# Fewer, area-weighted filler matmuls and softmax denominators spread by DMA, in a planned two-layer attention and MLP kernel

## The chip, the cores and the metric

The kernel runs on one core of one Trainium2 chip. The metric is the device time of one execution in microseconds (us). "Before" stands for the kernel as it is and "after" for the kernel with the change.

## The reference

Two layers are applied to one sequence of 2048 rows with 448 columns. Each layer is an attention block of 16 heads (28 columns each) and a mixer block with shifted groups of columns and an MLP of 1792 hidden columns. Each sub-block has a residual sum. Weights are the same in both layers.

```python
def _A_ref(x, wqkv, wo):                       # B=1, S=2048, D=448, H=16, Dh=28
    q, k, v = qkv of (x @ wqkv) by head
    p = softmax(einsum("bhqd,bhkd->bhqk", q, k) * Dh ** -0.5)
    return concat_heads(einsum("bhqk,bhkd->bhqd", p, v)) @ wo

def _B_ref(x, w1, w2, w3, w4):                 # F=1792
    h = gelu(layernorm(x) @ w1)
    hs = concat([h0 shifted by 1, h1 by -1, h2 by 2, h3 by -2]) @ w2   # four groups of 112 columns
    x1 = x + hs
    return x1 + gelu(layernorm(x1) @ w3) @ w4

for layer in range(2):
    x = x + _A_ref(layernorm(x), A_wqkv, A_wo)
    x = x + _B_ref(layernorm(x), B_w1, B_w2, B_w3, B_w4)
```

## The kernel before, in words

**A planner writes the order.** The kernel's Python holds tasks (generators such as `t_scores`, `t_exp`, `t_pv`, `t_norm`, `t_mixA`, `t_mixB`). Each task yields operations with an engine, a planned duration, and the tiles it reads and writes. `Sched.run` places them one after the other in planned time: the operation that can start first goes first, with priorities. The result is a fixed list for each of the five queues (TensorE `pe`, ScalarE `act`, VectorE `dve`, GpSimd `pool`, SyncE `sp`); each queue executes its list strictly in order and waits on semaphores where data come from another engine. So a planned duration that is wrong never makes the result wrong, but it puts operations at places in a queue where they are waited for.

**Filler.** `keep_pe_busy` looks at each gap in PE's planned list. Where the recent use of PE (planned busy time in the last `WIN` = 4.0 us) is at most `TARGET` = 0.8, it adds a filler: four matmuls of 256 columns on 32-column tiles of the array, into bank 6 or 7 of PSUM when it is free. Nobody reads what they write. In the list of instructions they are L1608.

**Attention.** Scores for four heads of a group (`g`) stand on four row tiles of the array (32 rows each, L1129). A unit of three or two PSUM banks (0 to 2 and 3 to 4) is turned into probabilities by one ACT instruction (L1204). The PV matmuls (L692, four column tiles) add into bank 5. A segment is one chunk of query rows (512, or 256 at the end), one group of four heads, and a range of key tiles; there are 64 segments. `ORDER` lists the ranges: the first chunks go over the keys in parts, since not all keys are there yet. At the end of a segment, VectorE moves bank 5 out, before the next segment's PV can start. Where a segment isn't its chunk's last one, the sum goes to DRAM (`uscr`) and comes back at the next part (`t_uload`), multiplied by a factor `fct` for the new maximum.

**Denominators.** Column 28 of each head's values is 1, so row 28 of each head's 32 rows of the sum is the softmax denominator. In the 36 final segments `t_norm` picks these rows with fp32 matmuls (`e28`), inverts them on VectorE (`rs`, L1335), turns them with another fp32 matmul (`identf`), copies them (`rT`, L1338), spreads them over the head's rows with fp32 matmuls (`selq`), and multiplies (L1342) into `otn`. An fp32 matmul is two records in the profile. The tile `u` (one buffer `u_sb`) is held from the copy out of bank 5 to this product; the part that is read back has one buffer, `uin`. Before the matmuls `t_norm` waits for `op_done`, the output projection of the chunk before, because `otn` has one buffer.

**After attention.** `t_outproj` multiplies by `wo` and adds to `x_res`. `t_mixA` and `t_mixB` are the mixer and the MLP for the tiles of a chunk: statistics on VectorE, the normalisation on GpSimd (`norm`, L845, into one of six `xn` tiles), a transposing DMA on SP (L850, `xT<-xn`), matmuls (L701), gelu on ACT (L1453 and L1569, each with a change of ACT's table). `t_ln1_l1` then normalises for the next layer, stores to `xnd`, and `load_xT` (L938) reads it back transposed for the projections `k_proj`, `q_proj`, `v_proj`. The projections square K and Q on GpSimd (L953, into one of three `sq` tiles) to bound the maximum of the scores.

Of the kernel before, what the change touches and what calls it, by code (L numbers as in the profile page):

```python
# [7 lines left out]
ALU = mybir.AluOpType  # L8
# [166 lines left out]
class Sched:  # L175
    LAT = 0.2
    EARLY = 0.25
    WIN = 4.0
    TARGET = 0.8
# [88 lines left out]
    def keep_pe_busy(self, until):  # L268
# [3 lines left out]
        while self.cur["pe"] + dur + 0.12 < until:  # L272
            t = self.cur["pe"]
            self.recent = [(a, b) for (a, b) in self.recent if b > t - self.WIN]
            used = sum(b - max(a, t - self.WIN) for (a, b) in self.recent)
# [15 lines left out]
            self.recent.append((t, t + dur))  # L291
# [4 lines left out]
    def run(self):  # L296
        P = self.P
        while True:
# [132 lines left out]
TR_T = 4.0  # L431
TRL_T = 6.0
# [21 lines left out]
def build_kernel(nc, A_x, A_wqkv, A_wo, B_x, B_w1, B_w2, B_w3, B_w4, out, n_layers=2):  # L454
    S = A_x.shape[1]
    D = 448
# [19 lines left out]
    NXN = 6  # L476
# [105 lines left out]
    with st:  # L582
# [39 lines left out]
        sq = sb("sq", [128, 3, 512], BF16)  # L622
# [18 lines left out]
        selq = sb("selq", [16, 512], FP32)  # L641
# [13 lines left out]
        SQ = ["sq0", "sq1", "sq2"]  # L655
        xst = h2T[:, :, :].rearrange("p a b -> p (a b)").rearrange("p (t d) -> p t d", d=D)

        def bi(b):
            return int(b[1:])

# [86 lines left out]
        def t_setup():  # L747
# [68 lines left out]
            yield op("dve", 0.5, lambda e: e.tensor_copy(out=selq[:, :].rearrange("p (c r) -> p c r", r=32), in_=identf[0:16, 0:16].unsqueeze(2).to_broadcast([16, 16, 32])),  # L816
# [138 lines left out]
        def k_proj(L, c, g, xt):  # L955
# [13 lines left out]
            if not fast:  # L969
                yield square(si, dst, dk)  # L970
# [8 lines left out]
        def q_proj(L, qc, g, xt):  # L979
# [8 lines left out]
            s = yield ("acq", SQ)  # L988
            si = num(s)
# [10 lines left out]
            if idx == 0 and g == 0:  # L1000
                yield square_first(b, si)
# [7 lines left out]
            else:  # L1009
                yield ("wait", ("bc", L, p0, g))  # L1010
                yield evac()
                yield ("rel", b)
                yield square(si, dst, [qk])
# [8 lines left out]
        def v_proj(L, c, xt):  # L1022
            yield ("wait", ("vinit",))
            for i in range(4):
# [3 lines left out]
                for fc in FCS:  # L1028
                    yield op("pe", c_mm(D), mm4(ps[:, bi(b), 0:D], xT[:, xt, fc, 128 * i:128 * i + 128], wv[:, fc, :], fc == 0, fc == 3),
# [86 lines left out]
        def score_ops(blks, banks):  # L1116
            m = max(len(seg_kb[b_[0]][b_[1]]) for b_ in blks)
            nc_ = len(blks)
            for i in range(m):
                for blk, bank in zip(blks, banks):  # L1120
# [4 lines left out]
                    if i >= len(ktl):  # L1125
# [6 lines left out]
                        reads=[("kT", g, vslot(L, kt)), qk], writes=[(("ps", bank), i) if len(ktl) > 1 else ("ps", bank)], mode="r32")  # L1132
# [118 lines left out]
        def t_pv():  # L1251
            yield ("wait", ("start",))
            yield ("acq", ["b5"])
            for si in range(len(segs)):
# [9 lines left out]
                while todo or dtodo:  # L1264
# [15 lines left out]
                    for kb in batch:  # L1280
                        for i, kt in enumerate(kbs[kb]):
                            vs = vslot(L, kt)
                            for j in range(4):
# [3 lines left out]
                                         reads=[("vaug", vs), (key, s)], writes=[(("ps", 5), j)], mode="col4")  # L1287
# [8 lines left out]

        def t_uload(si):
# [4 lines left out]
            yield ("acq", ["uin"])  # L1302
            k = 4 * (ch % 2) + g
            yield dma("sp", lambda e: e.dma_start(out=uin[:, :], in_=uscr[k]), reads=[("uscr", k)], writes=[("uin",)], t=3.0)
            yield ("sig", ("uin", si))

        def t_norm(si):
# [3 lines left out]
            yield ("acq", ["u"])  # L1311
            if first:
                yield op("dve", c_ps(NW), lambda e: e.tensor_copy(out=u_sb[:, 0:NW], in_=ps[:, 5, 0:NW]), reads=[("ps", 5)], writes=[("u",)])
            else:
                yield ("wait", ("uin", si))
                yield ("wait", ("fct", L, p[1]))
                yield op("dve", c_ps(NW), lambda e: e.scalar_tensor_tensor(out=u_sb[:, 0:NW], in0=uin[:, 0:NW], scalar=fct[:, L, p[1], g:g + 1], in1=ps[:, 5, 0:NW],  # L1317
                                                                            op0=ALU.mult, op1=ALU.add),
                         reads=[("ps", 5), ("uin",), ("fct", L, p[1])], writes=[("u",)])
                yield ("rel", "uin")  # L1320
            yield ("sig", ("ucopied", si))
            if not last:
                k = 4 * (ch % 2) + g
                yield dma("sp", lambda e: e.dma_start(out=uscr[k], in_=u_sb[:, :]), reads=[("u",)], writes=[("uscr", k)], t=3.0)
# [380 lines left out]
```

## Time and profile before

| | before |
|---|---|
| median of 3 runs | 1233.29 us (1232.92 to 1237.69) |
| profiled execution, its own time | 1229.68 us |
| its span, first to last instruction | 1227.9 us |
| PE busy, share of the span | 1115.2 us, 91% |
| ACT busy | 1062.9 us, 87% |
| DVE busy | 463.0 us, 38% |
| POOL busy | 344.4 us, 28% |
| mean granted TensorE clock | 0.947 |

All numbers of one profile come from one execution. PE is TensorE's matmuls, PEld its weight loads, which overlap them; DVE is VectorE, ACT ScalarE, POOL GpSimd, SP SyncE. A row of a group shows line, engine, operation, output and input tile, shapes and count, then busy time in us and the mean of one instruction in ns, then the idle time of that engine just before it and what ended it. A matmul's record includes its way through the array, so busy times of PE are more than the time for which it is filled. In the row PEclk and in tables by stage the granted clock is a share of full speed.

### The profile page before, as it was taken

To read this page: it belongs to the slowest core of one execution; us is meant where nothing else is said; L and a number is where in the kernel's file an instruction comes from. 1 tells how busy PE (TensorE), PEld (TensorE's weight loads), DVE (VectorE), ACT (ScalarE), POOL (GpSimd) and SP (SyncE) were. 2 spreads that over 40 slices of the span, in tenths; PEclk is the share of its full clock that TensorE was granted. 3 is DMA by queue.
4 is the path that set the end of the run, shared out by engine and by line. 5 is a ranking of instruction groups with operands and counts; after the bars stand their busy time and mean duration, and the time that the engine had idled before them with its cause. 6 is when DMAs were issued, how large, how long until landed. Compare 5 with 4: busy or idle time off the path is not lost.

```text
span 1227.9 us, 34609 instructions
## 1 busy us (share of the span) xinstructions
PE 1115.2 (91%) x15881; PEld 482.0 (39%) x15882; DVE 463.0 (38%) x985; ACT 1062.9 (87%) x906; POOL 344.4 (28%) x364
## 2 busy tenths in 40 slices
PE   5778999899989999899978998999989899989988
PEld 2223453344434433234323433354433333434454
DVE  7654212331232325431463343333343323333343
ACT  3767998999999999999968987999587999999942
POOL 4922203313224035510353231101334130341201
PEclk9889999899999999889988999999698999998999
DMA  3384102001010021100231120432211020120000
GB/s 100 79 229 102 49 10 36 6 11 55 18 32 19 2 81 34 31 5 11 76 78 51 32 80 26 108 95 74 43 27 23 2 52 2 42 42 10 11 17 21
DMA packets 90010, 55.95 MB, mean 46 GB/s; under 512 B 63945, under 2 KB 82249, under 8 KB 89865
## 3 DMA queue, kind: packets, MB, share of 16 engines
q1 hardware_dynamic: 86600, 49.27, 15.8%
q0 software_dynamic: 2304, 3.67, 1.2%
q8 instruction: 124, 2.03, 0.7%
q10 hardware_dynamic: 960, 0.80, 0.2%
q14 instruction: 22, 0.17, 0.1%
HBM read 20.30 MB, written 16.52 MB: 30 GB/s over the span
## 4 chain that ended last, share of the span: by engine, by line
PE 45%; ACT 33%; POOL 9%; DVE 8%; DMA 2%; SPq 2%; issue 2%; ACTq 0%; POOLq 0%; DVEq 0%
ACT PT L1204 28%; PE ps L701 21%; PE ps L692 11%; PE ps L1129 11%; POOL xn L845 5%; ACT h2T L1569 3%; PE ps L1608 2%; DVE st L830 1%; ACT hT L1453 1%; DVE h2T L1559 1%; DVE kmaxc L974 1%; ACT L1453 1%; ACT L1569 1%; DMA xT<-xn 1%; DVE x1b L1512 1%
## 5 line engine op out<-in xcount | busy, mean ns | idle before, releaser
L1204 ACT ACTIVATE PT<-ps 128x1536 bf16<-128x1536 f32 (+1 forms) x819 | 942.2, 1279 | 88.8 <-PE ps L1129 77.0
L1129 PE MATMUL ps<-qT,kT 32*128 32x512 bf16 (+1 forms) x2304 | 331.1, 370 | 16.1 <-ACT PT L1204 8.6
L692 PE MATMUL ps<-PT,vaug 128*32 128x512 bf16 (+1 forms) x2304 | 257.5, 374 | 0.8 <-DVE u_sb L1317 0.5
L1129 PEld LDWEIGHTS ps<-qT,kT 32*128 32x128 bf16 x2304 | 81.3, 91 | 285.1 <-ACT PT L1204 210.2
L701 PE MATMUL ps<-xT,w 128*32 128x512 bf16 (+2 forms) x2240 | 179.5, 371 | 11.9 <-DMA xT<-xn 5.3
L1608 PE MATMUL ps<-wq_pad,ident 128*32 128x256 bf16 x3632 | 170.5, 283 | 9.0 <-DVE x1b L1512 3.8
L701 PE MATMUL ps<-w,h2T 128*32 128x448 bf16 x1792 | 121.0, 370 | 10.4 <-ACT h2T L1569 10.4
L1608 PEld LDWEIGHTS ps<-wq_pad,ident 128*32 128x32 bf16 x3632 | 105.3, 99 | 42.7 <-issue 15.3
L1559 DVE CAST h2T<-ps 128x512 bf16<-128x512 f32 (+2 forms) x126 | 73.9, 587 | 113.7 <-PE ps L701 105.9
L692 PEld LDWEIGHTS ps<-PT,vaug 128*32 128x32 bf16 x2304 | 69.8, 96 | 95.7 <-issue 79.5
L701 PEld LDWEIGHTS ps<-xT,w 128*32 128x32 bf16 (+1 forms) x2240 | 60.2, 96 | 70.3 <-issue 43.1
L953 POOL TENSOR_TENSOR sq<-qT 128x512 bf16<-128x512 bf16 x31 | 32.2, 1039 | 141.2 <-DVE qT L996 140.3
L701 PEld LDWEIGHTS ps<-w,h2T 128*32 128x32 bf16 x1792 | 48.5, 99 | 56.0 <-issue 21.2
L836 POOL TENSOR_SCALAR vpe<-mv 128x1 f32<-128x1 f32 (+2 forms) x21 | 4.8, 229 | 229.3 <-DVE mv L831 229.3
L1569 ACT ACTIVATE h2T<-h2T 128x7168 bf16<-128x7168 bf16 (+2 forms) x9 | 45.1, 5016 | 16.0 <-DVE h2T L1559 15.9
L953 POOL TENSOR_TENSOR sq<-kT 128x512 bf16<-128x512 bf16 x31 | 32.2, 1041 | 94.1 <-DVE kT L965 94.0
L1410 POOL TENSOR_SCALAR mst<-mv 128x4 f32<-128x4 f32 (+1 forms) x9 | 2.2, 240 | 197.8 <-DVE mv L831 197.8
L701 PE MATMUL ps<-w,hT 112*32 112x448 bf16 x512 | 39.8, 421 | 18.8 <-ACT hT L1453 15.5
L845 POOL TENSOR_SCALAR xn<-x_res,mv,mst 128x448 bf16<-128x448 f32 x30 | 55.5, 1859 | 1.8 <-DVE mst L1416 1.5
L845 POOL TENSOR_SCALAR xn<-x1b,mv,mst 128x448 bf16<-128x448 f32 x29 | 54.4, 1876 | 1.3
L1516 POOL TENSOR_SCALAR mst<-mv 128x1 f32<-128x1 f32 x32 | 7.2, 226 | 167.9 <-DVE mv L831 167.9
L701 PE MATMUL ps<-xT,wk_pad 128*32 128x512 bf16 x512 | 46.0, 398 | 4.2 <-DVE kmaxc L974 3.5
(131 smaller groups left out, 1096.0 us busy)
## 6 DMA issues: line engine op xcount, KB each, us to landing
uscr<-u_sb SPq DMA_DIRECT2D x28, 256.0 KB, 2.4
uin<-uscr SPq DMA_DIRECT2D x28, 256.0 KB, 2.9
xnd<-xn SPq DMA_DIRECT2D x28, 128.0 KB, 1.7
x_res<-in_A_x_dram POOLq DMA_DIRECT2D x16, 224.0 KB, 2.7
xd<-x_res SPq DMA_DIRECT2D x16, 224.0 KB, 2.2
x_res<-xd SPq DMA_DIRECT2D x16, 224.0 KB, 3.8
out_dram<-obf SPq DMA_DIRECT2D x16, 112.0 KB, 1.7
w<-in_B_w_dram SPq DMA_DIRECT2D x1, 1568.0 KB, 14.1
```

What stands on the lines that cost most here:

```text
L692: return lambda e: e.matmul(out=out, lhsT=lhsT, rhs=rhs, start=start, stop=stop, **kw)
L701: r.append(e.matmul(out=out[c:c + w, :], lhsT=lhsT[:, c:c + w], rhs=rhs, start=start, stop=stop, tile_position=(0, c)))
L830: yield op("dve", 0.55, lambda e: e.bn_stats(out=st6[:, t, :], in_=src), reads=rkeys, writes=[("st6", t)])
L845: yield op(eng, dur, lambda e: e.tensor_scalar(out=xn[:, k, 0:D], in0=src, scalar1=scalar1, scalar2=scalar2, op0=ALU.subtract, op1=ALU.mul ...
L953: return op("pool", 1.2, lambda e: e.tensor_tensor(out=sq[:, si, :], in0=src, in1=src, op=ALU.mult), reads=rk, writes=[("sq", si)])
L974: yield op("dve", c_ps(512), lambda e: e.reduce_max(out=kmaxc[:, L, g, c:c + 1], in_=ps[:, bi(b2), :], axis=AX.X), reads=[("ps", bi(b2))], ...
L1129: yield op("pe", max(0.055, 0.22 / nc_ * NW / 512.0), lambda e, i=i, kc=kc, j=j, g=g, a=a, NW=NW, bank=bank: e.matmul(out=ps[:, bank, i * ...
L1204: yield op("act", 0.07 + n * 0.427, lambda e, bk=bk, s0=s0, n=n: e.activation(out=PT[:, s0:s0 + n, :], in_=ps[:, bk[0]:bk[0] + n, :], func ...
L1453: yield op("act", c_act(4 * NW), lambda e: e.activation(out=hT[0:112, :, c0:c0 + NW], in_=hT[0:112, :, c0:c0 + NW], func=ACT.Gelu_apprx_tanh),
L1559: ev = op("dve", c_ps(NW), lambda e, fch=fch, b=b: e.tensor_copy(out=h2T[:, fch, 0:NW], in_=ps[:, bi(b), 0:NW]), reads=[("ps", bi(b))], wr ...
L1569: yield op("act", c_act(14 * NW), lambda e: e.activation(out=h2T[:, :, 0:NW], in_=h2T[:, :, 0:NW], func=ACT.Gelu_apprx_tanh), reads=allk, ...
L1608: return [e.matmul(out=ps[32 * c:32 * c + 32, bi(b), 0:256], lhsT=ident[:, 32 * c:32 * c + 32], rhs=wq_pad[:, 0, 0:256], start=True, stop= ...
```

## The change

- The filler rule keeps a weight for each PE instruction. Scores and PV matmuls (a quarter of the array) count 512/9600 = 0.053 us, the filler 0.107 us, all others their planned duration. The window is 3.42 us and the target 0.5.
- In all final segments but the four of the last chunk, row 28 of each head goes by DMA from the sum to `rT` (16 x 128), VectorE inverts it there, a DMA stores it to a scratch in DRAM (`rscr`), and a third DMA reads it back with each row repeated 32 times into `rb`. GpSimd multiplies into `otn`. The wait for `op_done` stands only before this product.
- `u_sb` and `uin` become one tile with three buffers, `ub`; the part that is read back is updated in place.
- Planned durations: a norm on GpSimd 0.8 to 1.9 us, on VectorE 0.30 to 0.9; a transposing DMA from `xn` 4.0 to 3.0, from DRAM 6.0 to 5.0; fp32 matmuls of the last chunk 0.12 to 0.24, 0.23 to 0.29 and 0.25; a filler 0.13 to 0.12.
- `xn` has five tiles and not six, `sq` two and not three, and `sq` is taken after the projection has left PSUM, not before.

```diff
 class Sched:
-    WIN = 4.0
-    TARGET = 0.8
+    WIN = 3.42
+    TARGET = 0.5
...
     def keep_pe_busy(self, until):
-            self.recent = [(a, b) for (a, b) in self.recent if b > t - self.WIN]
-            used = sum(b - max(a, t - self.WIN) for (a, b) in self.recent)
+            self.recent = [x for x in self.recent if x[1] > t - self.WIN]
+            used = sum(w * (b - max(a, t - self.WIN)) / (b - a) for (a, b, w) in self.recent)
             if used > self.TARGET * self.WIN:
...
-            self.recent.append((t, t + dur))
+            self.recent.append((t, t + dur, 0.107))
...
-                self.recent.append((start, start + dur))
+                self.recent.append((start, start + dur, kw.get("w", dur)))
...
-TR_T = 4.0
-TRL_T = 6.0
+TR_T = 3.0
+TRL_T = 5.0
...
-    NXN = 6
+    NXN = 5
...
-        sq = sb("sq", [128, 3, 512], BF16)
+        sq = sb("sq", [128, 2, 512], BF16)
...
-        u_sb = sb("u_sb", [128, 512], FP32)
-        uin = sb("uin", [128, 512], FP32)
+        ub = sb("ub", [128, 3, 512], FP32)
+        rb = sb("rb", [128, 512], FP32)
...
+        rscr = nc.dram_tensor("rscr", (2, 4, 512), FP32).ap()
...
         def norm(eng, dst_slot, src, scalar1, scalar2, rkeys):
-            dur = 0.8 if eng == "pool" else c_f2b(D)
+            dur = 1.9 if eng == "pool" else 0.9
...
         def k_proj(L, c, g, xt):
-            s = yield ("acq", SQ)
-            si = num(s)
             fast = L == 0 and c == 0 and g == 0
             if fast:
+                s = yield ("acq", SQ)
+                si = num(s)
                 yield square_first(b, si)
...
             if not fast:
+                s = yield ("acq", SQ, dk)
+                si = num(s)
                 yield square(si, dst, dk)
...
         def t_uload(si):
-            yield ("acq", ["uin"])
+            u_ = yield ("acq", UB)
+            uin_of[si] = u_
...
         def t_norm(si):
-            yield ("acq", ["u"])
-            if first:
...
+            if not first:
                 yield ("wait", ("uin", si))
                 yield ("wait", ("fct", L, p[1]))
+                u_ = uin_of[si]
+            else:
+                u_ = yield ("acq", UB)
...
+            if (L, ch) != (1, len(CHUNKS[1]) - 1):
+                yield ("acq", ["rT"])
+                yield dma("sp", lambda e: e.dma_start(out=rT[0:4 * n, :], in_=ub[28:128:32, ui, 0:NW]), reads=[uk], writes=[("rT",)], t=2.2)
+                yield op("dve", 0.75, lambda e: e.reciprocal(out=rT[0:4 * n, :], in_=rT[0:4 * n, :]), reads=[("rT",)], writes=[("rT",)])
+                rk = si % 2
+                yield dma("sp", lambda e: e.dma_start(out=rscr[rk, :, 0:NW], in_=rT[0:4 * n, :]), reads=[("rT",)], writes=[("rscr", rk)], t=2.0)
+                yield ("rel", "rT")
+                yield ("acq", ["rb"])
+                yield dma("sp", lambda e: e.dma_start(out=rb[:, 0:NW], in_=rscr[rk, :, 0:NW].unsqueeze(1).to_broadcast([4, 32, NW])), reads=[("rscr", rk)], writes=[("rb",)], t=2.8)
+                if (L, ch) != (0, 0):
+                    pv = (L, ch - 1) if ch > 0 else (0, len(CHUNKS[0]) - 1)
+                    yield ("wait", ("op_done",) + pv)
+                yield op("pool", 0.2 + NW * 0.0021, lambda e: e.tensor_tensor(out=otn[:, g, 0:NW], in0=u, in1=rb[:, 0:NW], op=ALU.mult),
+                         reads=[uk, ("rb",)], writes=[("otn", g)])
+                yield ("rel", "rb")
+                yield ("rel", u_)
+                yield ("sig", ("norm", L, ch, g))
+                return
...
-        SC.fill = (0.13, filler, ["b6", "b7"], lambda b: ("ps", bi(b)), [("ident",), ("wq_pad",)])
+        SC.fill = (0.12, filler, ["b6", "b7"], lambda b: ("ps", bi(b)), [("ident",), ("wq_pad",)])
```

More of the change, by code (lines that the diff above doesn't have):

```diff
@@ L1286, in t_pv @@
                                                                    buf[:, s, i * NW:(i + 1) * NW], done == 0, done == total - 1, tile_position=(0, 32 * j)),
[L1287 removed]
+                                         reads=[("vaug", vs), (key, s)], writes=[(("ps", 5), j)], mode="col4", w=NW / 9600.0)
                             done += 1
@@ L1344, in t_norm @@
+            yield op("dve", c_ps(NW), lambda e: e.tensor_tensor(out=otn[:, g, 0:NW], in0=u, in1=ps[:, bi(b), 0:NW], op=ALU.mult),
+                     reads=[uk, ("ps", bi(b))], writes=[("otn", g)], touch=[b])
             yield ("rel", b)
-            yield ("rel", "u")
+            yield ("rel", u_)
             yield ("sig", ("norm", L, ch, g))
```

61 lines of the change are left out of this document (34 added, 27 removed).

## The prediction

> **What bounds the kernel now.** I read the engine shares first, then the groups of instructions and the waits for the idle time of the exponentials, then the table by stage for the stretches in which it falls.
>
> ```profile
> span 1227.9 us, 34609 instructions
> PE 1115.2 (91%) x15881; PEld 482.0 (39%) x15882; DVE 463.0 (38%) x985; ACT 1062.9 (87%) x906; POOL 344.4 (28%) x364
> L1204 ACT ACTIVATE PT<-ps 128x1536 bf16<-128x1536 f32 (+1 forms) x819 | 942.2, 1279 | 88.8 <-PE ps L1129 77.0 <-PE ps L692 9.1
> L1608 PE MATMUL ps<-wq_pad,ident 128*32 128x256 bf16 x3632 | 170.5, 283 | 9.0 <-DVE x1b L1512 3.8 <-POOL wq_pad L783 2.1 <-DVE otn L1342 1.5
> ACT fct L1104 <- DVE dbc L1099: 20.7, 4, 8.2
> 45.00:1175.00 1130.00, 1042.68 (x14624) 440.52 (x14625) 404.55 (x838) 1033.80 (x867) 310.12 (x317) 0.95 0.18 45
> ```
>
> The last row is a table by stage; its columns are length, then busy time with instruction count of PE, PE's weight loads, DVE, ACT and POOL, then granted clock, DMA share and GB/s. ACT holds the middle of the kernel: busy 1033.8 of the 1130 us between 45 and 1175. What can be won there is its 96.2 us of idling. The 45 us before and the 53 us after belong to loading, the first projections and the last tiles, which the change leaves nearly as they are. PE's 91% holds 170.5 us of filler (L1608) and is no bound by itself; it matters where a stalled matmul holds up the scores queued behind it. Most of the idling lies in a few places (the same table):
>
> ```profile
> 111.00:118.00 7.00, 4.62 (x106) 2.58 (x104) 6.19 (x20) 1.48 (x3) 2.33 (x3) 1.00 1.00 198
> 204.00:214.00 10.00, 8.57 (x83) 3.14 (x83) 2.39 (x4) 6.24 (x6) 1.04 (x1) 0.83 0.33 67
> 342.00:351.00 9.00, 7.61 (x85) 2.99 (x85) 2.39 (x4) 6.20 (x7) 1.04 (x1) 1.00 0.30 60
> 486.00:496.00 10.00, 8.85 (x93) 2.44 (x93) 3.08 (x6) 7.80 (x7) 0.00 (x0) 0.83 0.05 9
> 638.00:651.00 13.00, 10.44 (x122) 3.40 (x114) 2.81 (x4) 7.54 (x8) 4.71 (x5) 0.74 0.27 72
> 732.00:751.00 19.00, 15.24 (x132) 6.15 (x126) 12.29 (x36) 8.05 (x9) 2.08 (x2) 0.91 0.04 15
> 878.00:892.00 14.00, 13.33 (x84) 6.03 (x78) 2.66 (x5) 8.64 (x8) 1.28 (x3) 0.53 0.18 31
> 916.00:934.00 18.00, 16.72 (x134) 7.45 (x134) 5.26 (x13) 11.07 (x10) 8.62 (x10) 0.62 0.22 45
> 1104.00:1113.00 9.00, 7.90 (x85) 2.82 (x85) 1.59 (x4) 6.38 (x7) 0.00 (x0) 0.62 0.00 0
> ```
>
> **Step 1: one u tile and one uin tile become three shared tiles.** The 9.1 us wait on PE L692 (the PV matmuls) is one event. DVE in time order:
>
> ```profile
> 863.57 0.69 DVE L1342 TENSOR_TENSOR otn<-u_sb,ps 128x512 bf16<-128x512 f32 x1
> 864.36 0.75 DVE L1317 SCALAR_TENSOR_TENSOR u_sb<-uin,fct,ps 128x512 f32<-128x512 f32 x1
> 867.61 3.49 ACT L1204 ACTIVATE PT<-ps 128x1024 bf16<-128x1024 f32 x3 [9.14 <-PE ps L692]
> ```
>
> The finished segment held u_sb until its product at 863.57, because t_norm waits for the output projection of the chunk before. Only then could the next sum leave bank 5 (864.36), the PV matmuls go on and PT come free. With three tiles the next sum leaves at once. I take -8 us; bounds 0 and -9.1, as the third tile could itself be held by a reload.
>
> **Step 2: corrected durations in the planner.** The static order is made from durations in the code; these rows are their real sizes:
>
> ```profile
> L845 POOL TENSOR_SCALAR xn<-x_res,mv,mst 128x448 bf16<-128x448 f32 x30 | 55.5, 1859 | 1.8 <-DVE mst L1416 1.5
> xT<-xn SPq DMA_TRANSPOSE x59, 2.5
> 195.51 7.40 POOL L845 TENSOR_SCALAR xn<-x_res,mv,mst 128x448 bf16<-128x448 f32 x4 [0.31 <-DVE mst L1416]
> ```
>
> The old plan gives four POOL norms 4 x 0.8 and the transpose 4.0, so 7.2 us; the chip takes 7.4 + 2.5 = 9.9. PE's queue thus reaches the matmuls that need xT some 2.7 us early and scores wait behind them. The new plan says 4 x 1.9 + 3 = 10.6, late by 0.7 and harmless. Seven of the stretches above (204, 342, 486, 638, 878, 916, 1104) follow such a chain or the half clock after it. Their ACT idling is 3.76 + 2.80 + 2.20 + 5.46 + 5.36 + 6.93 + 2.62 = 29.1 us. Some is the real length of the chain, which no plan shortens, so I take 17 of it: -17, bounds 0 and -29. The stretches at 111 and 732 wait for key maxima through DVE (the fct wait, 20.7 us) and I leave them as they are.
>
> **Step 3: the fp32 matmuls go, in 32 of 36 final segments** (the last chunk keeps them).
>
> ```profile
> L692 PE MATMUL ps<-rT,selq 16*128 16x128 f32 (+1 forms) x256 | 44.6, 297 | 1.0 <-DVE rT L1338 0.7
> L692 PE MATMUL ps<-identf,rs 128*16 128x128 f32 (+1 forms) x72 | 14.6, 286 | 0.3 <-DVE rs L1335 0.3
> L692 PE MATMUL ps<-e,u_sb 128*128 128x4 f32 x256 | 38.1, 266 | 1.9 <-DVE x_res L1373 0.8 <-DVE hT L1479 0.6 <-DVE vaug L1033 0.3
> ```
>
> The last chunk's four segments have 16 + 8 + 16 = 40 of the 584 records, so 544/584 of 97.3 us, 90.6 us, leaves PE. ACT's exponentials cover nearly all of it. It counts only where scores are late already, with a few of these matmuls in each stall: -3 us, bounds 0 and -10. DVE loses a reciprocal, a copy and a product per segment, 32 x (0.26 + 0.28 + 0.69) by the rows in the next fence, and gains a reciprocal of 128 elements a lane. The rows of 16 and 8 elements, 257 and 206 ns, give 6.4 ns an element, so an estimate of 0.97 us. 39 us against 31; DVE has room (38%).
>
> **Step 4: the DMA chain instead.**
>
> ```profile
> 132.95 0.75 DVE L1317 SCALAR_TENSOR_TENSOR u_sb<-uin,fct,ps 128x512 f32<-128x512 f32 x1 [1.16 <-PE ps L692]
> 139.07 0.69 DVE L1342 TENSOR_TENSOR otn<-u_sb,ps 128x512 bf16<-128x512 f32 x1 [0.53 <-PE ps L692]
> L1335 DVE RECIPROCAL rs<-ps x36: 206/257/258, 135.9 to 1176.1; 128x16 f32<-128x16 f32 x28, 128x8 f32<-128x8 f32 x8
> L1338 DVE COPY rT<-ps x36: 272/279/280, 137.1 to 1177.3; 16x128 f32<-16x128 f32 x28, 8x128 f32<-8x128 f32 x8
> uscr<-u_sb SPq DMA_DIRECT2D x28, 256.0 KB, 2.4
> uin<-uscr SPq DMA_DIRECT2D x28, 256.0 KB, 2.9
> out_dram<-obf SPq DMA_DIRECT2D x16, 112.0 KB, 1.7
> L1527 POOL TENSOR_TENSOR x_res<-x_res,x1b 128x448 f32<-128x448 f32 x32 | 36.3, 1138 | 0.0
> ```
>
> Before, from the end of the copy (133.70) to the end of otn (139.76): 6.1 us. After: two small transfers at 2.0 each (between the 1.7 and 2.4 rows), 0.97, a spread of 256 KB at 2.9, a POOL product of 1.138 x 512/448 = 1.30: 9.2 us. So +3.1 us at each of the eight chunks that use it, through its last group. Attention of later segments hides it, except where layer 1 waits for layer 0's last chunk and where projections of short segments follow closely: +3, bounds 0 and 8 x 3.1 = +25.
>
> In the Trainium skill, "DMA: Bandwidth & Descriptors", section "Rules for kernel authors", a transfer is held to as many of the 16 engines as its slowest dimension allows. The spread reads four rows, so by that rule it has four engines; no run so far shows it.
>
> Queues: 32 products, 41.6 us, go on POOL (344 to 386 us), each waiting for its spread with norms and squares behind it. On SP 96 transfers are added, the reciprocal's store and the spread each waiting for the step before, with reloads of u and transposes behind. POOL is idle 72% of the time. I take +2, bounds 0 and +15, half a microsecond for each wait.
>
> **Step 5: the filler rule.** The granted clock halves for stretches of 3.41 us or a multiple:
>
> ```profile
> 365.43:368.85 3.42, 3.42 (x52) 1.26 (x48) 1.47 (x3) 3.42 (x4) 0.00 (x0) 1.00 0.00 0
> 368.85:372.26 3.41, 0.96 (x11) 0.21 (x8) 0.00 (x0) 3.38 (x3) 0.00 (x0) 1.00 0.00 0
> 372.26:375.67 3.41, 3.26 (x40) 1.49 (x44) 1.33 (x3) 3.38 (x4) 0.00 (x0) 0.50 0.00 0
> 201.59:205.01 3.42, 1.60 (x21) 0.52 (x19) 0.00 (x0) 3.19 (x4) 1.73 (x3) 1.00 0.41 79
> 205.01:208.42 3.41, 2.99 (x26) 0.76 (x26) 0.69 (x1) 0.51 (x1) 0.00 (x0) 0.50 0.75 154
> 157.22:160.64 3.42, 3.38 (x67) 1.80 (x65) 0.00 (x0) 3.42 (x4) 0.00 (x0) 1.00 0.02 5
> 157.22:160.64 3.42, 2.36 (x52) 1.57 (x52) 1.00 0.02 5
> sum 122.89, PE 115.34 PEld 44.13 DVE 40.89 ACT 86.63 POOL 27.87; mean PE 5.24 PEld 2.01 DVE 1.86 ACT 3.94 POOL 1.27
> ```
>
> The seventh row is the filler (L1608) alone; "sum" is over all half-clock stretches between 45 and 1175. A stretch of little PE work is followed by one at 0.50. In the attention-only window at 157, 52 of 67 matmuls are filler. Fillers stream 256 columns and the others 512, on a quarter of the array, so the filler does 52 x 256 of (52 x 256 + 15 x 512), 63%, of the work. The old target of 0.8 counts planned busy time: a pair of exponentials lasts 2.275 us in the plan, its scores and PV 0.44 + 0.275 = 31%, leaving 49% to filler. The new rule counts 10 x 0.0533 = 23% and stops at 50%, leaving 27%. At 0.107 and 0.13 us a group that is 2.5 groups per us against 3.8, so 3632 becomes some 2400 matmuls. In half-clock stretches ACT idles 36.3 of 122.9 us, elsewhere 59.9 of 1007.1, so a halved stretch costs (0.295 - 0.059) x 3.41 = 0.8 us. A few new ones in thin stretches against a few saved with step 2: +2 us, bounds -6 and +20 (25 new ones).
>
> In the Trainium skill, "TensorE: Matmul & The Clock Gate", section "Why this matters for your kernels", the advice is to leave no PE gap above about 3 us. The trace is stricter: the clock fell at 205 after a window with 1.60 us of PE work in it. By the page's rule the term is 0 and the sum 2 us lower.
>
> **Smaller edits.** Two sq tiles instead of three and five xn tiles instead of six are covered by taking sq only after the projection has left PSUM and by SP's prompt transposes; if that cover is gone the wait is that of the squares, 1 us each. Planned PE durations of the last chunk's matmuls change the order only. Zero for all.
>
> **Sum.** -8 - 17 - 3 + 3 + 2 + 2 = -21 us on the profiled execution's own 1229.7 (span 1227.9 and 1.8 around it), so 1208.7. The median of the runs shown, 1233.3, lies 3.6 above that, so I say **1212** (0.5%, some 6 us, is about what this kernel's measurement can tell).
>
> **Rivals.**
> - More: the new order removes nearly all of it, -9, -29, -6 and -6 for steps 1, 2, 3 and 5, with step 4 and the queues at 0: 1233.3 - 50 = 1183. For it: each stall is one PE queue entry placed too early. Against: part of each is the real length of its chain.
> - Nothing: stalls re-form elsewhere, so step 2 gives 0, the rest -4: 1229. For it: any new order moves every wait; the fct waits stay.
> - The spread is slow. From 1.7 us at 112 KB and 2.4 at 256 KB a transfer costs about 1.15 + 0.0049 per KB; on a quarter of the engines 256 KB takes 6.2 us, 3.3 more than I took. Over eight chunks at most 26 us, mostly hidden: +6, 1218. This is what the Trainium skill's rule on the slowest dimension would make of it.
> - Slower: the thinner filler lets the clock fall in attention-only phases. 23% there without filler, and execution runs behind the plan. Each new halved stretch costs 0.8 us; with 27 us to undo (21 and the 6 us bound) it decides from 34. With 45: +36, 1248. Against: 50% is twice the 23% that such a phase has by itself, and at 0.50 ACT still ran 70%.
>
> **Chances.** Forecast 0.48 (its own range 1198 to 1226), more 0.16, nothing 0.14, slow spread 0.10, slower 0.12. So faster 0.74, same 0.14, slower 0.12. The range runs from near the "more" case to the upper edge of "nothing": 1185 to 1236.
>
> **What would show it.** Step 1: no wait of ACT on L692 near 9 us. Step 2: the seven stretches after a POOL norm chain lose over half of their idling; ACT's wait on L1129 falls from 77 to about 55 us. Step 3: 40 fp32 records left. Step 4: the spread lands in about 2.9 us (6.2 by the rival), otn ends about 9 us after its segment's sum; POOL near 386 us. Step 5: about 2400 filler matmuls and a mean clock still between 0.94 and 0.96; below 0.93 the fourth rival holds. The prediction is wrong if ACT's idling does not shrink though POOL chains are planned rightly, or if the fct waits at layer 1 grow by more than step 4's few microseconds.

## The result, and the profile after

The changed kernel takes **1202.0 us** (median; 1197.8 to 1204.3) where the kernel before takes 1233.1: a ratio of 0.974, 95% interval 0.970 to 0.978. The forecast was 1212, with 1185 to 1236 as its range. The profiled execution took 1204.3 us against 1229.7 before, 25.4 less; in medians it is 31 less. All comparisons below use undisturbed runs.

The shares, the groups that carry the readings, two waits of ACT, and two tables by stage (the body from 45 us to the last exponentials, and the sum and mean over all half-clock stretches in it):

```profile
span 1202.5 us, 34008 instructions
PE 1058.9 (88%) x15542; PEld 417.7 (35%) x15542; DVE 452.2 (38%) x921; ACT 1059.7 (88%) x906; POOL 382.7 (32%) x396
L1643 PE MATMUL ps<-wq_pad,ident 128*32 128x256 bf16 x3836 | 182.4, 282 | 2.1 <-DVE x1b L1547 1.0 <-POOL wq_pad L788 0.5 <-DVE qT L1027 0.5
L1348 DVE RECIPROCAL rT<-rT 16x128 f32<-16x128 f32 (+1 forms) x32 | 30.0, 939 | 43.2 <-DMA rT<-ub 43.2
ACT PT L1213 <- PE ps L1138: 56.6, 51, 10.9
ACT fct L1113 <- DVE dbc L1108: 26.3, 3, 14.3
45.00:1146.00 1101.00, 978.81 (x14183) 373.24 (x14184) 391.08 (x765) 1028.26 (x865) 349.48 (x350) 0.96 0.22 54
sum 95.56, PE 86.94 PEld 28.77 DVE 25.09 ACT 73.34 POOL 17.33; mean PE 4.58 PEld 1.51 DVE 1.32 ACT 3.86 POOL 0.91
```

L1213 here is L1204 before, L1138 is L1129, L706 is L701, L697 is L692, L1643 is L1608, L850 is L845, L1113 is L1104. ACT idles 1101.0 - 1028.3 = 72.7 us in the body, 96.2 before: 23.5 us less, most of the 25.4. (Its busy time fell by 5.5 us there and the end piece grew by 3.6.) In half-clock stretches it idles 95.6 - 73.3 = 22.2 us (36.3 before), and at full clock some 51 (59.9 before). The wait for scores fell from 77.0 to 56.6 us, and the 9.1 us wait on the PV matmuls is gone.

So the total came out near the forecast. Two signs did not: 3836 filler matmuls stand where about 2400 were forecast, and the spread. Its first use, in order of time (start, duration, what, and the idle time before with what ended it):

```profile
125.55 0.67 SPq L1347 DMA_DIRECT2D rT<-ub  x1
127.76 0.93 DVE L1348 RECIPROCAL rT<-rT 16x128 f32<-16x128 f32 x1
128.72 0.34 SPq L1350 DMA_DIRECT2D rscr<-rT  x1
130.11 0.56 SPq L1353 DMA_DIRECT2D rb<-rscr  x1
135.40 1.27 POOL L1357 TENSOR_TENSOR otn<-ub,rb 128x512 bf16<-128x512 f32 x1 [2.19 <-DMA rb<-rscr]
```

From the issue of the spread to the product that needs it are 5.3 us, not 2.9. The chain of waits (shares of the span by what was waited for), of the kernel before and then of the changed one, shows what that does, and below it are pieces of the changed kernel's chain at layer 1, in order of time:

```profile
ACT PT L1204 28%; PE ps L701 21%; PE ps L692 11%; PE ps L1129 11%; POOL xn L845 5%; ACT h2T L1569 3%; PE ps L1608 2%; DVE st L830 1%; ACT hT L1453 1%; DVE h2T L1559 1%; DVE kmaxc L974 1%; ACT L1453 1%; ACT L1569 1%; DMA xT<-xn 1%; DVE x1b L1512 1%
ACT PT L1213 34%; PE ps L706 21%; PE ps L1138 9%; PE ps L697 6%; DMA rb<-rscr 4%; ACT h2T L1604 3%; POOL xn L850 2%; DMA xT<-xnd 1%; POOL otn L1357 1%; ACT hT L1488 1%; DMA rscr<-rT 1%; PE ps L1643 1%; DVE kmaxc L981 1%; DMA rT<-ub 1%; ACT L1604 1%
```

```profile
996.54 1.73 DMA rT<-ub
998.29 0.95 DVE rT L1348
999.26 1.38 DMA rscr<-rT
1000.71 5.11 DMA rb<-rscr
1005.88 1.28 POOL otn L1357
1007.21 0.59 PE ps L706 x3
```

POOL's norms fell from 5% of the chain to 2%, exponentials rose from 28% to 34%: the path runs along the bound more than before. But `rb<-rscr` is new on it with 4%, somewhat under 48 us. It is no longer hidden: here PE goes from the product straight into the output projection.

### The profile page after: what moved, and what is told of

Read it like the earlier page. It is cut to its first block, busy times and chain, and to the rows that moved or that the text cites. A ratio compares the mean times of both kernels' runs of the same rounds, so it can differ in the third digit from the quotient of the medians.

```text
span 1202.5 us, 34008 instructions
## 1 busy us (share of the span) xinstructions
PE 1058.9 (88%) x15542; PEld 417.7 (35%) x15542; DVE 452.2 (38%) x921; ACT 1059.7 (88%) x906; POOL 382.7 (32%) x396
## 3 DMA queue, kind: packets, MB, share of 16 engines
q1 hardware_dynamic: 92376, 57.63, 19.2%
## 4 chain that ended last, share of the span: by engine, by line
ACT 40%; PE 37%; DMA 8%; DVE 7%; POOL 5%; issue 1%; SPq 0%; ACTq 0%; POOLq 0%; DVEq 0%
ACT PT L1213 34%; PE ps L706 21%; PE ps L1138 9%; PE ps L697 6%; DMA rb<-rscr 4%; ACT h2T L1604 3%; POOL xn L850 2%; DMA xT<-xnd 1%; POOL otn L1357 1%; ACT hT L1488 1%; DMA rscr<-rT 1%; PE ps L1643 1%; DVE kmaxc L981 1%; DMA rT<-ub 1%; ACT L1604 1%
## 5 line engine op out<-in xcount | busy, mean ns | idle before, releaser
L1213 ACT ACTIVATE PT<-ps 128x1536 bf16<-128x1536 f32 (+1 forms) x819 | 939.3, 1307 | 59.2 <-PE ps L1138 56.6
L1138 PE MATMUL ps<-qT,kT 32*128 32x512 bf16 (+1 forms) x2304 | 326.5, 368 | 52.2 <-ACT PT L1213 43.6
L697 PE MATMUL ps<-PT,vaug 128*32 128x512 bf16 (+1 forms) x2304 | 254.1, 367 | 2.0 <-DVE ub L1335 2.0
L1138 PEld LDWEIGHTS ps<-qT,kT 32*128 32x128 bf16 x2304 | 80.3, 91 | 342.6 <-ACT PT L1213 271.7
L1643 PE MATMUL ps<-wq_pad,ident 128*32 128x256 bf16 x3836 | 182.4, 282 | 2.1 <-DVE x1b L1547 1.0
L706 PE MATMUL ps<-xT,w 128*32 128x512 bf16 (+1 forms) x2240 | 173.2, 367 | 6.9 <-issue 4.7
L706 PE MATMUL ps<-w,h2T 128*32 128x448 bf16 x1792 | 123.5, 382 | 20.8 <-ACT h2T L1604 20.8
L1357 POOL TENSOR_TENSOR otn<-ub,rb 128x512 bf16<-128x512 f32 (+1 forms) x32 | 38.6, 1205 | 320.6 <-DMA rb<-rscr 314.1
L1643 PEld LDWEIGHTS ps<-wq_pad,ident 128*32 128x32 bf16 x3836 | 108.9, 98 | 43.3 <-issue 23.8
L697 PEld LDWEIGHTS ps<-PT,vaug 128*32 128x32 bf16 x2304 | 69.8, 95 | 102.1 <-issue 85.4
L706 PEld LDWEIGHTS ps<-xT,w 128*32 128x32 bf16 x2240 | 59.0, 96 | 63.8 <-issue 38.1
L706 PEld LDWEIGHTS ps<-w,h2T 128*32 128x32 bf16 x1792 | 49.7, 102 | 68.6 <-issue 27.3
L850 POOL TENSOR_SCALAR xn<-x_res,mv,mst 128x448 bf16<-128x448 f32 x30 | 55.6, 1865 | 1.9 <-DVE mst L1451 1.9
L850 POOL TENSOR_SCALAR xn<-x1b,mv,mst 128x448 bf16<-128x448 f32 x29 | 54.5, 1879 | 1.7 <-POOL mst L1553 0.2
L1333 DVE COPY ub<-ps 128x512 f32<-128x512 f32 (+1 forms) x36 | 22.7, 630 | 85.4 <-PE ps L697 85.2
L706 PE MATMUL ps<-w,hT 112*32 112x448 bf16 x512 | 40.9, 414 | 13.8 <-ACT hT L1488 13.5
L706 PE MATMUL ps<-xT,wq_pad 128*32 128x512 bf16 x512 | 44.8, 420 | 6.2 <-DMA xT<-xnd 5.5
L706 PE MATMUL ps<-wo_pad,otn 128*32 128x448 bf16 x512 | 42.0, 378 | 9.1 <-POOL otn L1357 6.1
```

The costliest lines, as they stand in the source:

```text
L697: return lambda e: e.matmul(out=out, lhsT=lhsT, rhs=rhs, start=start, stop=stop, **kw)
L706: r.append(e.matmul(out=out[c:c + w, :], lhsT=lhsT[:, c:c + w], rhs=rhs, start=start, stop=stop, tile_position=(0, c)))
L850: yield op(eng, dur, lambda e: e.tensor_scalar(out=xn[:, k, 0:D], in0=src, scalar1=scalar1, scalar2=scalar2, op0=ALU.subtract, op1=ALU.mul ...
L1138: yield op("pe", max(0.055, 0.22 / nc_ * NW / 512.0), lambda e, i=i, kc=kc, j=j, g=g, a=a, NW=NW, bank=bank: e.matmul(out=ps[:, bank, i * ...
L1213: yield op("act", 0.07 + n * 0.427, lambda e, bk=bk, s0=s0, n=n: e.activation(out=PT[:, s0:s0 + n, :], in_=ps[:, bk[0]:bk[0] + n, :], func ...
L1333: yield op("dve", c_ps(NW), lambda e: e.tensor_copy(out=u, in_=ps[:, 5, 0:NW]), reads=[("ps", 5)], writes=[uk])
```

## The experiments

Each ratio is to the kernel before, measured again beside each group of runs, with its 95% interval. Differences in us are differences of these ratios times 1233 us. First each part alone, on the kernel before.

**Durations alone.**

```diff
-TR_T = 4.0; TRL_T = 6.0
+TR_T = 3.0; TRL_T = 5.0
...
-            dur = 0.8 if eng == "pool" else c_f2b(D)
+            dur = 1.9 if eng == "pool" else 0.9
```

> The kernel before with only the planned durations corrected (norms 1.9 and 0.9, transposes 3.0 and 5.0). Theory A, that PE's entries stood too early after GpSimd's norms: 12 to 20 us less than before, and the stalls after norm chains more than halved. Theory B, that the gain comes from taking the fp32 matmuls off PE: within 5 us of before. Theory C, that any new order moves the time by chance: anything between -12 and +12 us, with the stalls at other places but not shorter.

Measured: 1215.9 us, 0.986 (0.983 to 0.990), -17 us. Its groups still show the long wait on PV, as no u tile was added:

```profile
L1204 ACT ACTIVATE PT<-ps 128x1536 bf16<-128x1536 f32 (+1 forms) x819 | 939.5, 1294 | 67.6 <-PE ps L1129 55.8 <-PE ps L692 8.5
```

The wait for scores fell by 21.2 us, from 77.0 to 55.8. The prediction's sign was that the seven stretches after a POOL norm chain lose over half of their idling. Here are the seven together before, then stretches of the same lengths at the same distance behind the same chains, with durations alone and in the changed kernel:

```profile
sum 83.00, PE 73.42 PEld 28.24 DVE 20.18 ACT 53.87 POOL 16.68; mean PE 10.49 PEld 4.03 DVE 2.88 ACT 7.70 POOL 2.38
sum 83.00, PE 80.01 PEld 35.52 DVE 22.26 ACT 69.98 POOL 24.54; mean PE 11.43 PEld 5.07 DVE 3.18 ACT 10.00 POOL 3.51
sum 83.00, PE 76.46 PEld 25.76 DVE 26.97 ACT 74.69 POOL 29.06; mean PE 10.92 PEld 3.68 DVE 3.85 ACT 10.67 POOL 4.15
```

ACT's idling there, 83.0 less its busy time, falls from 29.1 us to 13.0 and 8.3, so the sign came out, although one of the seven kept its idling in the run alone (5.4 us before, 6.5 here). Planned durations alone are a real gain, with the same work, and theory A holds. They have a cost too: ACT's waits for `fct` grow from 20.7 to 30.7 us.

**Filler rule alone.**

```diff
-    WIN = 4.0; TARGET = 0.8
+    WIN = 3.42; TARGET = 0.5
... weights: scores and PV NW / 9600.0, filler 0.107, others their duration
```

> The kernel before with only the filler rule changed (weights, window 3.42, target 0.5, planned 0.12). Theory A: within 6 us of before, with about as many half-clock stretches (36 of 3.41 us between 45 and 1175). Rival, that the filler rule carries the gain through the clock: 10 us or more less, and under 25 such stretches. Filler matmuls: some 2400 by the prediction; above 3600 if the weights free more time than the lower target takes.

Measured: 1253.8 us, 1.019 (1.016 to 1.022), +23 us. Groups, the sum over half-clock stretches, and three neighbouring stretches of about 3.4 us (the second row of 147.50 is the filler alone):

```profile
L1608 PE MATMUL ps<-wq_pad,ident 128*32 128x256 bf16 x2284 | 111.9, 290 | 6.4 <-DVE x1b L1512 3.2 <-DVE otn L1342 1.6 <-DVE obf L1593 1.2
sum 187.75, PE 180.36 PEld 69.44 DVE 47.44 ACT 132.22 POOL 32.33; mean PE 7.21 PEld 2.78 DVE 1.90 ACT 5.29 POOL 1.29
144.10:147.50 3.40, 2.87 (x46) 1.11 (x44) 0.69 (x1) 3.40 (x4) 3.06 (x5) 1.00 0.48 122
147.50:150.96 3.46, 2.94 (x30) 1.58 (x30) 1.00 (x2) 3.30 (x5) 0.00 (x0) 1.00 0.70 195
147.50:150.96 3.46, 0.41 (x8) 0.20 (x6) 1.00 0.70 195
150.96:154.37 3.41, 3.41 (x25) 1.49 (x18) 0.28 (x1) 3.23 (x3) 0.00 (x0) 0.50 0.09 31
```

2284 fillers and 55 halved stretches (187.75 / 3.41) against 36 before; ACT idles 55.5 us in them. Neither expectation foresaw a loss; the forecast's fourth rival did. The stretch at 147.50 has PE busy for 2.94 of 3.46 us, yet it is followed by a half clock. The one before it is busy for only 2.87 of 3.40 us, but with 46 matmuls and not 30, and the clock stays. So the busy share of PE does not decide here. That it is the number of columns streamed, on a quarter of the array, is argued from such counts and not shown.

**Three u tiles alone**, with the denominators still by matmul. For room the tile `PD`, which no instruction uses here, is made smaller. Two segments can now be in their denominators at once and share `rs` and `rT`, so denominators of neighbouring segments can mix; the run is read for its time only.

```diff
-        u_sb = sb("u_sb", [128, 512], FP32)
-        uin = sb("uin", [128, 512], FP32)
+        ub = sb("ub", [128, 3, 512], FP32)
```

> The kernel before with only three shared u tiles, and denominators by matmuls as before (an unused tile is made smaller for the room). Theory A: 7 to 10 us less, and no wait of ACT on PV matmuls near 9 us. Theory B: within 4 us of before, as the stall then moves to the next wait. Theory C: as in the durations run.

Measured: 1216.8 us, 0.988 (0.986 to 0.991), -14 us; the profiled execution stands at 1218.8, 10.9 under that of before. The stretch that held the 9.1 us wait, before and then with three tiles:

```profile
845.00:870.00 25.00, 23.71 (x278) 10.22 (x275) 14.09 (x31) 15.82 (x14) 5.44 (x6) 0.88 0.08 23
845.00:870.00 25.00, 24.03 (x266) 11.01 (x264) 14.91 (x33) 23.95 (x22) 7.69 (x8) 0.94 0.05 12
```

ACT is busy 23.95 of 25 us there instead of 15.82: 8.1 us from the one event. That is theory A's mechanism; the whole gain is 4 us over its range.

**DMA denominators, with three u tiles,** the old durations and the old filler rule. The edit is step 4's chain and step 1's tiles, with `TR_T`, `TRL_T`, `norm`, `WIN` and `TARGET` of before (and `PD` as in the run above).

> The kernel before with the three u tiles and the denominators by DMA, old planned durations and old filler rule. Theory A: 5 to 12 us less, nearly all of it the u tiles' part. Theory B: 18 to 28 us less, PE busy some 50 us lower. Theory C: as in the durations run.

Measured: 1234.0 us, 0.999 (0.996 to 1.003). Against the three tiles alone the DMA chain loses 0.011 of the time, some 13 us, and ACT's wait for scores rises above that of before:

```profile
L1209 ACT ACTIVATE PT<-ps 128x1536 bf16<-128x1536 f32 (+1 forms) x819 | 940.2, 1295 | 106.0 <-PE ps L1134 104.3
PE ps L706 <- DMA xT<-xn: 20.6, 5, 5.2
```

PE waits 20.6 us for the transposed norms, 5.3 before and 11.9 with the three tiles alone. Before four of these five waits the norms themselves were no slower than before the change: POOL ran the four of a chain back to back in 7.4 us, as in the first row below, with no product between them. What stood between was on SP: other transfers went out among the transposes. The longest wait is for a product, and the other rows, from POOL, SP and PE, show how it comes about:

```profile
199.25 7.40 POOL L850 TENSOR_SCALAR xn<-x_res,mv,mst 128x448 bf16<-128x448 f32 x4 [0.31 <-DVE mst L1447]
882.21 7.41 POOL L850 TENSOR_SCALAR xn<-x_res,mv,mst 128x448 bf16<-128x448 f32 x4
884.11 3.03 SPq L855 DMA_TRANSPOSE xT<-xn  x2
887.18 0.52 SPq L1349 DMA_DIRECT2D rb<-rscr  x1
892.24 1.26 POOL L1353 TENSOR_TENSOR otn<-ub,rb 128x512 bf16<-128x512 f32 x1 [2.05 <-DMA rb<-rscr]
893.55 0.56 PE L706 MATMUL ps<-wo_pad,otn 128*32 128x448 bf16 x4 [8.69 <-POOL otn L1353]
```

The spread stands on SP behind two transposes, and these wait for norms that the plan takes for 0.8 us each. The product comes late, and PE stands 8.7 us before the output projection; in the changed kernel the longest such wait is 3.6 us. So the DMA chain and the norms share two queues, and a norm planned too short makes the chain late. Whether these waits are all of the 13 us is not shown. Theories A and B both missed; theory C, chance, allows this time too, and the run with the old durations in the whole, below, speaks against it.

**Filler rule with small weights for the fp32 matmuls.** Why did the rule lose 23 us? The plan counts the fp32 matmuls of a final segment as some 1.6 us of use, though they hold few columns.

```diff
-  ... reads=[("u",), ("e28",)], writes=[("ps", bi(b))], touch=[b])
+  ... reads=[("u",), ("e28",)], writes=[("ps", bi(b))], touch=[b], w=0.01)
   (identf and selq matmuls: w=0.02)
```

> The filler run again (the kernel before with only the filler rule), but the fp32 matmuls of the denominators count with the weights 0.01 and 0.02 us that the change gives those of its last chunk, not with their planned 0.12 and 0.23. Theory D, that the new rule starved the ends of segments because the plan took the fp32 matmuls for work that keeps the clock up: half-clock stretches back from 55 to 40 or fewer, and the time within 8 us of before. Rival E, that a target of 0.5 is too thin everywhere: still 50 stretches or more and 15 us or more over before.

Measured: 1247.6 us, 1.011 (1.007 to 1.015); 2472 fillers, 52 halved stretches, clock 0.926. By the ratios 0.0073 of the time, 9 of the 23 us, comes back. The number of stretches is as rival E said, and the loss of 14 us just under its 15. So the counting of the fp32 matmuls is the smaller part, and most of the loss is the thin filler itself.

Then the parts within the whole.

**After, with the old filler rule** (4.0, 0.8, planned durations).

> The changed kernel with the old filler rule (window 4.0, target 0.8, planned busy time, planned 0.13). Theory D: without the fp32 matmuls the rule hardly matters, so within 8 us of the changed kernel, with 5000 or more filler matmuls. Rival E: 10 to 20 us less than the changed kernel, as the new rule costs here what it cost alone. Rival F, that the old rule's filler now stands in the way of scores: 10 us or more over the changed kernel, as in the run with DMA alone, which gained nothing though it had three u tiles.

Measured: 1193.7 us, 0.967 (0.964 to 0.970). The new rule costs 8 us in the whole too, between theory D and rival E. Filler and half-clock stretches:

```profile
L1643 PE MATMUL ps<-wq_pad,ident 128*32 128x256 bf16 x5772 | 256.4, 279 | 0.7 <-POOL wq_pad L788 0.2 <-DVE qT L1027 0.2 <-DVE h2T L1594 0.2
sum 68.26, PE 61.52 PEld 21.55 DVE 23.89 ACT 49.87 POOL 9.63; mean PE 4.73 PEld 1.66 DVE 1.84 ACT 3.84 POOL 0.74
```

20 halved stretches instead of 28. With the fp32 matmuls gone, the old rule puts in 5772 instead of 3632, and the new one 3836 instead of 2284. In both kernels the new rule thus removes a good third; the freed room raised both counts.

**After, with the old durations** (4.0, 6.0, 0.8).

> The changed kernel with the old planned durations (norms 0.8 and 0.30, transposes 4.0 and 6.0). Theory A: 12 to 20 us over the changed kernel, in the stretches after norm chains. Rival, that the parts don't add: within 6 us of it, or 25 us or more over it.

Measured: 1235.8 us, 1.001 (0.998 to 1.004): the whole gain is gone. ACT's group, and the wait of PE:

```profile
L1213 ACT ACTIVATE PT<-ps 128x1536 bf16<-128x1536 f32 (+1 forms) x819 | 940.9, 1299 | 104.1 <-PE ps L1138 102.1
PE ps L706 <- DMA xT<-xn: 22.5, 6, 4.9
```

In the changed kernel that wait of PE on `xT<-xn` is 1.5 us. The durations are worth 34 us in the whole and 17 alone, as in the rival, by which the parts don't add: the DMA chain needs them. Here too the longest wait of PE is for a product on POOL, 9.6 us.

**After, with the spread as four transfers**, one for each head.

```diff
-  ... e.dma_start(out=rb[:, 0:NW], in_=rscr[rk, :, 0:NW].unsqueeze(1).to_broadcast([4, 32, NW])) ... t=2.8)
+  for j4 in range(4):
+      ... e.dma_start(out=rb[32*j4:32*j4+32, 0:NW], in_=rscr[rk, j4:j4+1, 0:NW].to_broadcast([32, NW])) ... t=2.8)
```

> The changed kernel with the spread as four transfers, one for each head (a row repeated over 32 partitions), in place of one that reads four rows. Theory G, that a slowest dimension of four holds the transfer to a quarter of the engines: from the issue of the first to the start of the product under 4 us, against 5.3 in the changed kernel, although three more issues of half a microsecond stand before it; time 0 to 6 us less. Rival: still 5 us or more, the time within 4 us, as the latency is the same and the issues cost what is won.

Measured: 1184.3 us, 0.959 (0.955 to 0.962), 18 us faster than the changed kernel. Its timeline and chain:

```profile
129.79 1.72 SPq L1354 DMA_DIRECT2D rb<-rscr  x4
133.19 1.27 POOL L1358 TENSOR_TENSOR otn<-ub,rb 128x512 bf16<-128x512 f32 x1 [0.29 <-DMA rb<-rscr]
ACT PT L1213 41%; PE ps L706 20%; PE ps L1138 8%; PE ps L697 6%; ACT h2T L1605 4%; POOL xn L850 2%; ACT hT L1489 1%; DVE kmaxc L981 1%; ACT L1605 1%; ACT L1489 1%; DMA rscr<-rT 1%; DMA xT<-xnd 1%; DVE st L835 1%; DMA xT<-xn 1%; DVE kT L970 1%
```

The product starts 3.4 us after the first issue instead of 5.3, and `rb<-rscr` has left the largest entries of the chain. The Trainium skill's rule ("DMA: Bandwidth & Descriptors", "Rules for kernel authors"), that a transfer gets no more engines than its slowest dimension allows, agrees: four transfers of 32 rows each move the same 256 KB sooner than one whose outer dimension is 4. How many engines each used is not measured. Theory G was right about the time to the product, but the gain in the whole is three times what it allowed. The plan changed too: it issues one transfer per 0.1 us, so it now expects the last row after 3.1 us, close to the 3.4 measured, where it was 2.5 us short before.

**After, with the slow spread planned at its real length.** Is it the latency that costs 18 us, or the plan's wrong idea of it? One number changes and the transfer stays one:

```diff
-  ... writes=[("rb",)], t=2.8)
+  ... writes=[("rb",)], t=5.3)
```

> The changed kernel with its one slow spread, planned at the 5.3 us that it takes and not at 2.8. Theory H, that the slow spread costs through the order (the output projection's matmuls stand in PE's queue some 2.5 us before otn is there): 10 to 18 us less than the changed kernel, nearly all that the four transfers won. Rival, that the latency itself or the load on four engines costs: within 5 us of the changed kernel.

Measured: 1183.1 us, 0.958 (0.955 to 0.961), as fast as with four transfers. The transfer is as slow as ever:

```profile
129.65 0.55 SPq L1353 DMA_DIRECT2D rb<-rscr  x1
134.91 1.27 POOL L1357 TENSOR_TENSOR otn<-ub,rb 128x512 bf16<-128x512 f32 x1 [2.16 <-DMA rb<-rscr]
ACT PT L1213 <- PE ps L1138: 42.6, 44, 10.9
ACT PT L1213 40%; PE ps L706 22%; PE ps L1138 9%; PE ps L697 7%; ACT h2T L1604 3%; DMA rT<-ub 1%; PE ps L1643 1%; DMA xT<-xnd 1%; ACT hT L1488 1%; DMA xT<-xn 1%; DVE kmaxc L981 1%; ACT L1604 1%; ACT L1488 1%; DVE vaug L1042 1%; DVE h2T L1594 1%
```

5.3 us from issue to product, yet the chain no longer lists it and ACT waits 42.6 us for scores instead of 56.6. The cost lay in what the plan put behind a transfer it took for 2.8 us, not in the transfer. Little of it is PE's own wait for the products, which fell from 6.1 to 4.0 us; the rest lies in other entries of the order.

**Four transfers and the old filler rule together.**

> The changed kernel with the four-transfer spread and the old filler rule, the two edits that each won (18 and 8 us). If they add: some 1176 us. If the filler rule only mattered where the order was wrong: within 4 us of the four-transfer run.

Measured: 1175.8 us, 0.952 (0.948 to 0.957), the fastest version: 26 us under the changed kernel, which is 18 + 8. The two parts add. What is left of the half clock, 10 stretches, and the longest `fct` wait, as in the changed kernel:

```profile
sum 34.14, PE 33.66 PEld 13.58 DVE 15.88 ACT 28.34 POOL 5.63; mean PE 4.21 PEld 1.70 DVE 1.99 ACT 3.54 POOL 0.70
ACT fct L1113 <- DVE dbc L1108: 26.3, 3, 14.3
```

**After, with the old filler rule and the denominators by matmul** (one segment at a time holds `rs` and `rT`), as the counterpart of the run with the old filler rule.

> The changed kernel with the old filler rule and the denominators by matmuls again (one segment at a time between the inversion and the product): planned durations and three u tiles remain. If the parts add as they did alone (17 and 14 us): some 1202, so 8 us over the same kernel with DMA (1194). Theory B, that taking the fp32 matmuls off PE is worth more: 1210 or over. Rival, that the DMA chain with its late spread eats what it wins: 1194 or less.

Measured: 1222.1 us, 0.989 (0.986 to 0.991). Against the 0.967 of the run with DMA denominators that is 27 us slower, as theory B said (1210 or over). But it is no faster than durations alone (0.986), though it has three tiles, so the lock on `rs` and `rT` may have a large part in these 27 us, which no run separates. Runs without the lock give a safer comparison, all with the old filler rule. Three tiles and DMA chain together moved the time by 1 us with the old durations (0.999), and by 24 us with the corrected ones (0.967 against 0.986 for durations alone; the smaller edits are in these 24 us). So what the chain is worth does depend on the durations.

**After, nudged.** How much does a meaningless change of order move the time? The planner's `LAT` goes from 0.2 to 0.21.

> The changed kernel with the planner's latency between engines at 0.21 us and not 0.20: nothing of the work changes, only the order by small steps. It tells how far a chance change of the order moves the time. If the parts measured are worth their face value: within 5 us of the changed kernel. Theory C: 8 us or more off, in either direction.

Measured: 1197.1 us, 0.969 (0.965 to 0.974), 5 us from the changed kernel, the edge of the first expectation. It is one such change, so others may move the time more. Differences of some 5 us between two plans therefore say nothing of the part that was edited; the 8 us of the filler rule in the whole is not far above that, and leans on the run of the rule alone.

## Why the prediction was right, and where its terms were not

| step | forecast | alone | within the whole |
|---|---|---|---|
| 1, three u tiles | -8 (0 to -9.1) | -14 | not tried |
| 2, durations | -17 (0 to -29) | -17 | -34 |
| 3 and 4, fp32 matmuls out, DMA chain in | +2 (-3 + 3 + 2) | +13 | -27, with the lock |
| 5, filler rule | +2 (-6 to +20) | +23 | +8 |
| sum | -21 | +5 | -31 measured |

- **The total and the sign were right, by the term that carried them.** Step 2 alone gave 17 us (12 to 21 by its interval), in the stretches that the prediction named, and without it nothing is left. ACT's wait for scores fell to 56.6 (forecast 55). ACT's waits were the right place to look: 23.5 of 25.4 us came from its idling. That alone it is 17 and not 12 or 21 is luck, as 17 was picked between 0 and 29; in the whole it is 34, beyond that bound.
- **Step 1 was about right.** The event gave 8.1 us, as worked out. The 3 to 6 us above it (11 between the profiled executions, 14 by the ratios) are no more than the idle nudge moved, so they say nothing of the tiles.
- **Steps 3 and 4 had the wrong structure.** They were costed by themselves, with attention as cover. The reciprocal (0.97 forecast, 0.94 measured) and POOL's busy time (386 and 382.7) were right. But the spreads stand on SP among the transposes and the products on POOL among the norms, so the chain's cost depends on the durations that step 2 corrects: +13 us with wrong durations, and with right ones tiles and chain win 24 together. The sum has only +2 for these queues, half a microsecond for each wait, and no term for the interaction.
- **The spread was mis-sized.** 2.9 us was taken from a 256 KB reload, 5.3 was measured, nearest the third rival's 6.2. From the sum's end to the end of the product, in the piece at layer 1, are 1007.16 - 996.52 = 10.6 us. That is only 1.4 more than the 9.2 forecast, as the small transfers took 1.73 and 1.38 instead of 2.0 each. The rival priced the slowness at +6 us because it would be mostly hidden. In the plan as written some 18 us hung on it, through the order: planned at 5.3 us, the slow spread is as good as four faster transfers.
- **Step 5 failed in count and price.** 2400 fillers is right for the rule on the kernel before (2284), but step 3 frees planned use, and the sum did not carry that over: 3836. Its +2 was +23 alone. The price of a halved stretch held: 19 new ones added 55.5 - 36.3 = 19.2 us of idling in half-clock stretches, 0.2 of each being what ACT idles at full clock too. At 0.8 us each they are 15 of the 21 us between the profiled executions. Their number was wrong: about 15 stretches beyond the few foreseen, against 25 in the bound. The fourth rival's mechanism is thus real and present in the changed kernel (28 halved stretches against 20 with the old rule), only outweighed.
- **What was to be left as it was.** The `fct` waits of both layers together rose from 20.7 to 26.3 us, the longest from 8.2 to 14.3. The prediction named growth at layer 1 as a sign against it, and there the sum hardly moved: 4.9 and 8.2 us before, one wait of 14.3 after. But the sum put these waits at no change, and step 2 changes them. The longest is 12.8 us or more in every run with the corrected durations, and 8.2 or less in every run with the old ones. The rows are for durations alone, for the changed kernel with the old durations, and for the stretch of the changed kernel's long wait, in which ACT is busy 8 of 25 us:

```profile
ACT fct L1104 <- DVE dbc L1099: 30.7, 4, 12.8
ACT fct L1113 <- DVE dbc L1108: 13.2, 3, 5.4
708.00:733.00 25.00, 19.88 (x212) 7.87 (x204) 16.84 (x45) 7.99 (x9) 6.04 (x5) 0.93 0.08 28
```

Why the new order lengthens it stays open. It stands in the fastest version too, and is the next thing to work on.

So the prediction is right for its main reason, while errors of both signs cancelled: alone, steps 5 and 3 with 4 were 21 and 11 us dearer than forecast and step 1 was 6 cheaper, and between the sum of the parts alone (+5) and the whole (-31) lie 36 us of interaction, of which 17 show as the difference between step 2 alone and in the whole. That these errors left the total within 10 us of the forecast is luck. What stays open: which of the entries behind the spread carry the 18 us, how much of step 1's gain remains in the whole, and what the smaller edits do (`xn`, `sq`, the last chunk's planned matmuls), which no run has alone.

## What to carry to other kernels

In a kernel whose queues are filled from a plan, measure every planned duration first: a wrong one can cost more than the operation's own time, and a change that adds work to a misplanned chain can lose alone and win once the plan is right. Here a late transfer on the chain of waits was cured as well by planning it late as by making it fast. Cost parts of such a change in pairs where they share a queue, and do not read differences of the size that an idle nudge makes.

## What the runs showed of the hardware

- The clock fell although PE was nearly always busy: 2.94 us of PE work in 3.46 with 30 matmuls, then 0.50; after 2.87 us in 3.40 with 46 matmuls it stayed at 1.00. In the Trainium skill, "TensorE: Matmul & The Clock Gate", section "Why this matters for your kernels", the advice is about gaps of some 3 us; here all gaps together were 0.52 us, so short gaps did not keep the clock. How the share of the array enters is argued from the counts, not measured by itself.
- A 256 KB spread whose source has four rows took 5.1 us on the chain, a plain 256 KB reload 2.9; as four transfers, with 1.72 us of issue, it let its product start after 3.4.
- Fewer fillers (2284 for 3632) beside the same other work lowered the mean clock from 0.947 to 0.923; in the changed kernel more of them (5772 for 3836) raised it from 0.956 to 0.971. The denser filler did not hold up the scores: ACT's wait for them was 50.5 us with 5772, and 56.6 with 3836.
